# Other PSUM buffers for the turned x, and grams held next to their posts, in a kernel of RWKV-6 attention and an MLP-mixer

## The chip, the cores and the metric

The kernel runs on one core of one Trainium2 chip. The metric is the device time of one execution in microseconds (us), as the median of several runs. A program on one core has no die to compare with, so a run counts as fast when it is within 1.5% of the fastest run of its kernel. The engines are called as in the profile: PE is TensorE, PEld its weight loads, DVE is VectorE, ACT is ScalarE, SP is SyncE.

## The reference

Four batches of a recurrent attention are followed by an MLP-mixer. All inputs are fp32.

```python
# B=4, H=8 heads, S=768, D=48; d_model = 384
for t in range(S):
    cur = einsum('bhd,bhe->bhde', u[None] * kt, vt)
    y[:, :, t] = einsum('bhd,bhde->bhe', rt, state + cur)
    state = wt[:, :, :, None] * state + einsum('bhd,bhe->bhde', kt, vt)
x = y.transpose(0, 2, 1, 3).reshape(B, S, H * D)
# mixer: d_tok = 256, d_ch = 1536
h = maximum(x.transpose(0, 2, 1) @ w_tok1, 0) @ w_tok2
u = x + h.transpose(0, 2, 1)
out = u + maximum(u @ w_ch1, 0) @ w_ch2
```

The kernel works the recurrence in blocks. Within a piece of 256 tokens, six "levels" each compute a gram (products of k and r in small tiles of the TensorE array), and an engine picks the wanted entries out of it. A "post" then transposes k (kT), forms the state increments (kv), updates the states, and forms y from the states and from the picked grams. The mixer of one batch (h, turned x, z, q products) is woven with the attention of the next batch, so that small-tile and full-size products share TensorE.

## The kernel before

The program keeps its PSUM tiles in three pools, eight banks in all; a bank here is 512 columns of fp32 in the tiles as declared (a gram's is [128, 2, 512]). The names in quotes are the tags by which tiles share buffers.

```python
ps_g = ctx.enter_context(tc.tile_pool(name="ps_g", bufs=2, space=bass.MemoryType.PSUM))  # 2 x 2 banks: "gram"
ps_a = ctx.enter_context(tc.tile_pool(name="ps_a", bufs=1, space=bass.MemoryType.PSUM))  # 1 x 2 banks: kv, y: "a"
ps_m = ctx.enter_context(tc.tile_pool(name="ps_m", bufs=2, space=bass.MemoryType.PSUM))  # 2 x 1 bank: all else: "m"
```

The mixer's turning stage makes one h product and one turn of x for each of six chunks of 128 tokens. Both take an "m" buffer. VectorE empties the h buffer, ScalarE empties the turn's.

```python
def back(c):
    ps = ps_m.tile([128, DM], f32, name="h_ps", tag="m")
    for i in range(DTOK // 128):
        pe.matmul(ps, wtok2[:, i, ts(c, 128)], h1[:, i, :], ...)
    dve.tensor_add(x[:, c, :], x[:, c, :], ps)

def turn(c):
    ps = ps_m.tile([128, DM // 128, 128], f32, name="xT_ps", tag="m")
    for m in range(DM // 128):
        pe.transpose(ps[:, m, :], xs[bt][:, c, ts(m, 128)], ident)
    act.copy(xT[:, :, ts(c, 128)], ps)
```

The post's transposes of k also take "m" buffers, except in the first batch, where a gram buffer holds both halves.

```python
def tokens():
    ...
    if bt == 0:
        both = ps_g.tile([128, 2, 512], f32, name="gram").rearrange("p c (a t) -> p c a t", a=A)
    for c in range(UC):
        ps = both[:, c] if bt == 0 else ps_m.tile([128, A, 128], f32, name="kT_ps", tag="m")
        for a in range(A):
            pe.transpose(ps[:, a, :], k_[:, ts(c * A + a, 128)], ident)
        act.copy(L["kT"][:, c], ps)
```

One post is joined with the levels of the piece after it. A scheduler then decides the order on TensorE: it may place a gram's products in front of, among or behind the products that they are joined with.

```python
def one(*pieces):
    return (sum(c for c, _ in pieces), lambda: emit(pieces))

return [begin, tokens, one(carry, first), update, one(before, rest[0]), one(within, rest[1]), *loads, *rest[2:]]
```

Here `carry` makes kv, `first` the level-0 gram (gram0), `before` the part of y from the states, `rest[0]` the level-1 gram, `within` the part of y from the picked grams, `rest[1]` the level-2 gram.

## Time and profile before

| | before |
|---|---|
| time, median of 3 runs | 627.08 us (625.52 to 629.18) |
| span of the profiled run | 624.1 us |
| TensorE busy | 591.5 us, 95% |
| TensorE's share of the chain that ended last | 88% |
| VectorE's share of that chain | 6% |
| visits to the small tiles on TensorE (counted in the built order) | 86 |

The prediction below shows the page, the last batch's turning stage, a stretch with attention and a kT stage. One more place of the kernel before matters later: a turning stage of a middle batch, which has attention beside it. This is the chain in order of time; the columns are start in us, length in us, and what ran.

```profile
394.23 0.71 PE y_ps L370 x22
394.94 1.49 PE h_ps L428 x4
396.43 0.33 PE xT_ps L435 x3
396.76 0.38 PE y_ps L370 x16
397.13 1.50 PE h_ps L428 x4
```

TensorE never rests in these lines. Yet the y products come in scraps of 22 and 16, each scrap a visit to the small tiles of its own, and four h matmuls take 1.49 us instead of the 4 x 0.323 = 1.29 us of an undisturbed row. The scraps stand where an h product waits for an "m" buffer to be emptied. By the timeline ScalarE's copy of the turn came last at the first of these two h products (394.27 to 394.75 us), and VectorE's add at the second (396.47 to 397.02).

### The profile page before, as it was taken

The numbers are of one execution on the slowest core, as the hardware profiler recorded it, in microseconds if no ns is written. First come the engines' busy times: TensorE is split into PE (matmuls) and PEld (weight loads), VectorE is DVE, ScalarE is ACT, GpSimd is POOL, SyncE is SP. The second block draws the span as 40 slices with busy tenths as digits, with TensorE's granted clock in tenths as the row PEclk, the third lists the DMA queues.
The fourth block names the chain that finished last, engine by engine and source line by source line (L and its number), as shares of the span: only waits on it lengthen the run. The fifth ranks groups of instructions, "written<-read, shape, count | busy, mean of one in ns | idle before, by whom it ended". The sixth has DMA issues, their size and how long they took to land.

```text
span 624.1 us, 19852 instructions
## 1 busy us (share of the span) xinstructions
PE 591.5 (95%) x8980; PEld 500.7 (80%) x8980; DVE 341.5 (55%) x743; ACT 201.6 (32%) x500; POOL 7.2 (1%) x32
## 2 busy tenths in 40 slices
PE   2888788999999999999999999999999999999997
PEld 2867556876888896789889896789899885898987
DVE  5889799996766783436364362526243331040403
ACT  6064554520355433432323312332212411202020
POOL 4000000000000000000000000000000000000000
PEclk9996679999999999999999999999999999999999
DMA  8236564610232222111111100000000000000000
GB/s 344 105 80 213 162 197 141 221 43 27 65 94 79 54 67 66 30 50 27 53 45 60 27 28 27 1 2 3 26 2 27 2 27 1 0 1 26 16 12 26
DMA packets 19380, 38.63 MB, mean 62 GB/s; under 512 B 2112, under 2 KB 12864, under 8 KB 19296
## 3 DMA queue, kind: packets, MB, share of 16 engines
q1 hardware_dynamic: 19152, 37.36, 19.0%
q8 instruction: 70, 1.15, 0.8%
q14 instruction: 14, 0.11, 0.1%
q10 hardware_dynamic: 144, 0.00, 0.0%
HBM read 32.64 MB, written 4.72 MB: 60 GB/s over the span
## 4 chain that ended last, share of the span: by engine, by line
PE 88%; DVE 6%; ACT 3%; issue 1%; DMA 1%; SPq 0%; DVEq 0%; ACTq 0%
PE z_ps L443 30%; PE q_ps L477 25%; PE gram L256 8%; PE h_ps L428 5%; PE h_ps L421 5%; PE h_ps L453 3%; PE y_ps L383 2%; PE y_ps L370 2%; PE kv_ps L333 2%; PE gram L233 2%; PE kT_ps L323 1%; PE xT_ps L435 1%; PE gram L250 1%; DVE state L350 1%; DMA w<-in_rkw_dram 1%
## 5 line engine op out<-in xcount | busy, mean ns | idle before, releaser
L443 PE MATMUL z_ps<-xT,wch 128*128 128x256 f32 x864 | 195.3, 382 | 0.0
L443 PEld LDWEIGHTS z_ps<-xT,wch 128*128 128x128 f32 x864 | 161.4, 190 | 22.4 <-ACT z L445 0.7
L445 ACT ACTIVATE z<-z_ps 128x256 f32<-128x256 f32 x144 | 55.0, 382 | 159.4 <-PE z_ps L443 145.7
L477 PE MATMUL q_ps<-wch,z 128*128 128x192 f32 x528 | 93.6, 329 | 0.0
L477 PEld LDWEIGHTS q_ps<-wch,z 128*128 128x128 f32 x528 | 86.3, 190 | 1.3
L477 PE MATMUL q_ps<-scratch,z 128*128 128x192 f32 x396 | 71.1, 330 | 0.0
L256 PEld LDWEIGHTS gram<-r,k 48*64 48x64 f32 x3072 | 59.4, 153 | 13.0 <-issue 7.2
L256 PE MATMUL gram<-r,k 48*64 48x32 f32 x3072 | 64.6, 235 | 4.1 <-issue 1.8
L477 PEld LDWEIGHTS q_ps<-scratch,z 128*128 128x128 f32 x396 | 64.3, 190 | 0.9 <-ACT kT L324 0.2
L288 DVE TENSOR_TENSOR k<-k,decay 112x512 f32<-112x512 f32 x36 | 24.9, 691 | 46.1 <-PE gram L256 34.6
L469 DVE TENSOR_TENSOR z<-z 128x768 f32<-128x768 f32 x11 | 10.5, 958 | 63.5 <-ACT z L445 63.4
L288 DVE TENSOR_TENSOR k<-k,w 112x512 f32<-112x512 f32 x36 | 24.8, 690 | 35.6 <-PE gram L256 30.0
L428 PE MATMUL h_ps<-h,wtok 128*128 128x384 f32 x96 | 37.0, 510 | 3.8 <-DVE x L430 2.0
L350 DVE SCALAR_TENSOR_TENSOR state<-state,w_chunk,kv_ps 128x48 f32<-128x48 f32 x160 | 30.7, 258 | 17.3 <-PE kv_ps L333 17.3
L421 PE MATMUL h_ps<-x,wtok 128*128 128x384 f32 x96 | 37.5, 541 | 1.7 <-ACT x L389 1.6
L430 DVE TENSOR_TENSOR x<-x,h_ps 128x384 f32<-128x384 f32 x24 | 13.3, 555 | 36.6 <-PE h_ps L428 36.3
L233 PE MATMUL gram<-rp,kp 48*64 48x64 f32 x768 | 22.5, 248 | 10.9 <-ACT kp L221 8.2
L272 DVE COPY_PREDICATED at<-mask,gram 128x512 f32<-128x512 uint8 x36 | 32.3, 898 | 0.0
L233 PEld LDWEIGHTS gram<-rp,kp 48*64 48x64 f32 x768 | 18.4, 154 | 15.4 <-ACT kp L221 10.7
L421 PEld LDWEIGHTS h_ps<-x,wtok 128*128 128x128 f32 x96 | 19.2, 208 | 13.5 <-ACT x L389 2.0
L280 ACT COPY at<-gram 16x256 f32<-16x256 f32 x48 | 17.4, 363 | 36.3 <-PE gram L256 35.1
L428 PEld LDWEIGHTS h_ps<-h,wtok 128*128 128x128 f32 x96 | 16.4, 189 | 15.5 <-DVE x L430 3.3
(80 smaller groups left out, 563.0 us busy)
## 6 DMA issues: line engine op xcount, KB each, us to landing
scratch<-in_w_ch_dram SPq DMA_DIRECT2D x10, 512.0 KB, 4.4
vt<-in_v_dram SPq DMA_DIRECT2D x12, 384.0 KB, 3.7
out_dram<-o SPq DMA_DIRECT2D x24, 192.0 KB, 1.9
x<-in_w_ch_dram SPq DMA_DIRECT2D x8, 512.0 KB, 4.4
w<-in_rkw_dram SPq DMA_DIRECT2D x18, 192.0 KB, 3.3
k<-in_rkw_dram SPq DMA_DIRECT2D x18, 192.0 KB, 3.1
r<-in_rkw_dram SPq DMA_DIRECT2D x18, 192.0 KB, 3.5
scratch<-in_w_tok_dram SPq DMA_DIRECT2D x4, 512.0 KB, 9.2
```

The lines of the kernel that those rows point to most:

```text
L233: pe.matmul(g[cols, q, ts(a, T)], L["kp"][rows, tokens], L["rp"][rows, tokens], start=True, stop=True)
L256: fours(lambda q, j, rows, cols: pe.matmul(g[cols, q, ts(ca, 32)], k_[rows, ds(ca * 128 + j * T, T)], right[rows, ts(2 * ca + j, 32 // b), ...
L272: dve.copy_predicated(out=dst, data=g.rearrange("p q (m b) -> p q m b", b=b), mask=masks[l].rearrange("p x t -> p (x t)").rearrange("p (m ...
L280: act.copy(at[p:p + b, :, :, n * 2 * b + b:(n + 1) * 2 * b], g[p:p + b, :, :, ts(n, b)])
L288: dve.tensor_mul(left, left, wv[:, :, 1].unsqueeze(2).to_broadcast([ROWS, n, b]))
L350: dve.scalar_tensor_tensor(new[:, a], state[bt, g][:, a], L["w"][:, c, a, j:j + 1], got[:, a], op0=ALU.mult, op1=ALU.add)
L421: pe.matmul(sums[i], wtok1[:, c, ts(i, 128)], xs[bt][:, c, :], start=(c == 0), stop=(c == C - 1))
L428: pe.matmul(ps, wtok2[:, i, ts(c, 128)], h1[:, i, :], start=(i == 0), stop=(i == DTOK // 128 - 1))
L443: pe.matmul(ps, wch1[:, m, ts(jt, 128)], xT[:, m, ts(s, SEG)], start=(m == 0), stop=(m == DM // 128 - 1))
L445: act.activation(zs[s][:, jt, :], ps, AF.Relu)
L453: pe.matmul(ps, zs[0][:, jt, ts(n, 128)], wch2[:, jt, :], start=(jt == 0), stop=(jt == NJ - 1))
L477: pe.matmul(ps, a[:, j, :], b[:, j, :], start=(j == 0), stop=(j == HJ - 1))
```

## The change

It has two parts. The first moves the turned x out of the two "m" buffers: in the first and the last batch to the buffer of kv and y, in the middle batches to the gram buffers. The second holds a gram's products behind the last TensorE product of the piece that it is joined with, by a dependency in the scheduler that is declared `NoSync`. Its aim is one joint visit to the small tiles instead of several scraps.

```diff
+    block = nc.cur_bb.bb
+    no_sync = mybir.DependencyInfo(mybir.DependencyClass.NoSync, mybir.DependencyReason.DATA)
+
+    def products(f):
+        done = len(block.instructions)
+        f()
+        return [ins for ins in block.instructions[done:] if ins.engine == pe.engine]
 ...
         def turn(c):
-            ps = ps_m.tile([128, DM // 128, 128], f32, name="xT_ps", tag="m")
+            if bt in (0, B - 1):
+                ps = ps_a.tile([128, 2, 512], f32, name="xT_ps", tag="a")
+            else:
+                ps = ps_g.tile([128, 2, 512], f32, name="xT_ps", tag="gram")
+            ps = ps[:, 0, :DM].rearrange("p (m t) -> p m t", t=128)
 ...
+        def both(f, g):
+            behind = products(f)[-1].name
+            for ins in products(g):
+                tc.add_manual_dep(ins, behind, no_sync, reason="products in tiles together")
+
         def one(*pieces):
-            return (sum(c for c, _ in pieces), lambda: emit(pieces))
+            return (sum(c for c, _ in pieces), lambda: both(*(f for _, f in pieces)))
```

## The prediction

> **What bounds the kernel now.** I read the page first: busy shares, slices, chain by line.
>
> ```profile
> PE 591.5 (95%) x8980; PEld 500.7 (80%) x8980; DVE 341.5 (55%) x743; ACT 201.6 (32%) x500; POOL 7.2 (1%) x32
> PE   2888788999999999999999999999999999999997
> PEclk9996679999999999999999999999999999999999
> PE 88%; DVE 6%; ACT 3%; issue 1%; DMA 1%; SPq 0%; DVEq 0%; ACTq 0%
> ```
>
> TensorE is the bound from about 90 us on: 88% of the chain that ended last is TensorE, the granted clock is full there, VectorE is at 55%. But 95% busy does not mean that TensorE has nothing to lose. The chain in order of time shows what a matmul costs in a row: 72 z matmuls in 15.54 us (216 ns each), 84 q matmuls in 13.65 us (163 ns), 24 h matmuls in 7.74 us (323 ns), three transposes in 0.33 us. (One fp32 matmul of the program is two instructions, a transpose is one.) Anything above these is a wait or a change of tile size. Here is the last batch's turning stage (520 to 533 us) in that view; columns are start, length, what:
>
> ```profile
> 523.72 1.57 PE h_ps L428 x4
> 525.29 0.02 issue
> 525.31 0.56 DVE x L430
> 525.88 0.04 issue
> 525.92 1.57 PE h_ps L428 x4
> ```
>
> A chunk takes 525.92 - 523.72 = 2.20 us, while its work is 4 x 0.323 + 0.33 = 1.62 us. The missing 0.58 us is the next h product waiting for VectorE's add to empty its PSUM buffer: h products and turns alternate in the two "m" buffers, so each h product gets the buffer that the one before it just left. The timeline says the same: "idle 0.32" before that matmul, though its row counts as busy nearly throughout.
>
> Now a stretch with attention beside it:
>
> ```profile
> 194.92 2.79 PE z_ps L443 x12
> 197.70 1.08 PE y_ps L383 x64
> 198.78 0.92 PE gram L256 x64
> 199.70 2.79 PE z_ps L443 x12
> 202.49 1.06 PE gram L256 x64
> ```
>
> 64 small-tile products cost 1.06 to 1.08 us when they open a visit to the 64-row tiles, 0.92 us when they follow others; 12 z matmuls after a visit take 2.79, not 12 x 0.216 = 2.59 us. So one visit costs 0.14 + 0.20 = 0.34 us beyond its work. Last, a kT stage:
>
> ```profile
> 331.93 0.44 PE kT_ps L323 x4
> 332.37 0.26 PE gram L233 x2
> 332.63 0.59 PE kT_ps L323 x4
> 333.21 0.26 PE gram L233 x4
> 333.47 4.10 PE q_ps L477 x24
> ```
>
> Six gram instructions cost 0.52 us in two visits; inside a longer visit one costs about 0.0145 us (0.92/64).
>
> [...] here the h matmul's row says 510 ns while one starts each 323 ns. [...]
>
> **The change, part by part.** No operation is added or removed: 4574 matmuls in both programs. Comparing the two built orders, the changes between full and small tiles on TensorE fall from 173 to 127, so visits from 86 to 63. All orders are the same up to the first batch's turning stage (about 92 us).
>
> (a) Turns of the first and last batch move to the buffer of kv and y, free at that time. The h products then own both "m" buffers. Last batch: the stage runs from 520.29 to 533.15, 12.86 us; 24 x 0.323 + 18 x 0.109 = 9.71; of the difference 0.2 us is the restart at its head and stays: gain 2.95. First batch: from the first transposes (92.72) to the first z (103.73) 11.01 us; 16 x 0.323 + 18 x 0.109 = 7.13; gain 3.88. VectorE also converts weights here; laying its 0.55 us adds and 0.4 to 0.7 us conversions in the new order against chunks of 1.62 us, each add is ready before the turn that wants it (the add of a chunk has 1.62 us, a turn plus an h product). I take 3.8.
>
> (b) Turns of the two middle batches move to the gram buffers. Their waits were filled with scraps of gram and y, 22 instructions or so at a time. From first transposes to first z: 11.55 us (249.20 to 260.75) and 11.2 us (391.1 to 402.3). After: 7.13 + one visit of 48 y and 64 gram. Alone 48 y cost 1.06 as 64 do, gram behind them 0.92, restart 0.20: 2.2. That is 9.33 us. In the first of the two, 38 y of the next visit also come back from the scraps: +0.5; and one turn stands behind the gram's pick in the ring (k and r products and pick, 0.69 + 0.69 + 1.30 us, then an add of 0.55, against about 3.2 us of TensorE work): +0.3. Gains 1.4 and 1.85.
>
> (c) One visit in the first batch's attention (gram at 166.97, y at 168.88) becomes joint: 0.34.
>
> (d) Eight kT stages lose 15 small visits (14 fewer in the count, as one stays as part of a longer visit). At 0.34 us this would be 4.8 us, but I do not believe it: these scraps stand in waits. At 331.93 the second half of kT needs the buffer that VectorE's L503 (331.97, 0.35 us) empties: it could start at 332.40 by the timeline, against 332.56. The next q needs the buffer that ScalarE empties at 333.04, about 333.1 against 333.40. So 0.3 us of that stage is won. Done alike for the eight (three at 0.3, five at 0 to 0.1, those where kT waits for VectorE's k product or for a ScalarE queue full of picks): 1.15 us. The 112 gram instructions moved into the kv visits cost 112 x 0.0145 = 1.6 us there. Net -0.45.
>
> Sum: 2.95 + 3.8 + 1.4 + 1.85 + 0.34 - 0.45 = 9.9 us; 627.1 - 9.9 = 617.2 us.
>
> **Rivals.** First: (d) pays as designed, all visits at 0.34 us. For it: TensorE is the bound and the costs are exact to a hundredth. Against: the idle times named above. It would make 612 us. Second: held grams bring new waits. y must now come before its gram, and y waits for the state updates: where gram used to go first (218.79), y started at 219.43 just as VectorE ended the last update (219.4). In the new order it would be asked for at about 219.4, so 0 to 0.3 us each in three places; if the picks behind also slip, 2 to 3 us and 620. Third: the first batch's 3.8 us are given back, because VectorE is busy all of 104 to 135 us with conversions. Against: the last block of the first channel weight is written by 112.8 us, and the matmuls that read it start at about 124.5; the second weight is complete at 132.6, needed some 8 us after 135. Slack of over 8 us against 3.8. If wrong: 621. Fourth: sharing the gram ring stalls the turns of the middle batches (or the grams behind them), (b) gives nothing: 620.5.
>
> **Range and chances.** Rival one alone reaches 2% (below 614.5), and I give it one in ten. Slower by 2% would need 12 us of new waits that nothing in the orders shows. The runs of before spread over 3.7 us, so ±2 us is noise between sets. Range 613.8 to 620.6; faster by over 2% 0.09, within 2% 0.90, slower 0.01.
>
> **What would show it.** (a) The chain between 520 and 533 us should have no VectorE add, with chunks 1.62 us apart; likewise in the first batch. (b) One gram-and-y visit in each middle turning stage, and perhaps a short wait before the fifth turn of the second batch. (c, d) kT stages of eight transposes in a row with a wait between the halves and one behind, of 0.2 to 0.4 us, about as long as the scraps were; kv and gram in one visit of about 2.2 us. Wrong would be: kT stages without those waits (then 612), or new idle time before y or before turns (then 620).

## The result, and the profile after

| | before | after |
|---|---|---|
| time, median of 6 runs each on one chip | 626.71 us (625.52 to 629.18) | 618.60 us (617.19 to 619.60) |
| ratio of fast runs | | 0.9865, 95% interval 0.9843 to 0.9887 |
| span of the profiled run | 624.1 us | 617.1 us |
| visits to the small tiles | 86 | 63 |

A ratio here is the mean time of one kernel's fast runs over the mean of the other's in the same rounds, so it is not quite the ratio of the medians quoted beside it. 1.35% is less than 2%; the interval shows that the gain is real. The predicted time was 617.2 us and the range 613.8 to 620.6.

First the page of the kernel after: busy time by engine, the granted TensorE clock in 40 slices, and the shares of the chain that ended last.

```profile
PE 587.0 (95%) x8980; PEld 499.0 (81%) x8980; DVE 341.2 (55%) x743; ACT 201.1 (33%) x500; POOL 7.2 (1%) x32
PEclk9999679999999999999999999999999999999999
PE 86%; DVE 6%; ACT 3%; DMA 2%; issue 2%; SPq 0%; ACTq 0%; DVEq 0%
```

The busy share of TensorE is 95% as before, although 7 us of the span are gone. The share tells nothing of this change, because a part of the waits counts as busy: of the 0.58 us missing in each chunk of the prediction's turning stage, only 0.32 show as idle. The counts of these instructions are the same; the granted clock is 1.00 from 90 us on in both (windows of 90 to 617 us here and of 90 to 623 us before).

The last batch's turning stage, chain in order of time:

```profile
519.32 1.29 PE h_ps L437 x4
520.61 0.33 PE xT_ps L449 x3
520.94 1.29 PE h_ps L437 x4
522.23 0.33 PE xT_ps L449 x3
```

Chunks are 520.94 - 519.32 = 1.62 us apart instead of 2.20, VectorE's add is no longer in the chain, and four h matmuls take the 1.29 us of an undisturbed row.

The middle batch's turning stage (the one shown above of before):

```profile
395.84 0.33 PE xT_ps L449 x3
396.17 0.89 PE y_ps L379 x42
...
397.23 0.93 PE gram L265 x59
398.15 0.48 PE xT_ps L449 x3
```

The scraps of y and gram have become one visit, with y first and gram behind it (where they meet, a few start times mix).

A kT stage:

```profile
330.56 0.45 PE kT_ps L332 x4
...
331.09 0.59 ACT kT L333
...
331.73 4.17 PE q_ps L491 x24
```

The grams that stood here before are gone, and nothing has taken their place. The q product after the transposes waits until ScalarE's copy (331.09 to 331.69) has emptied the "m" buffer of the first half. TensorE needs 0.44 us for each half, so it is idle for 331.73 - 330.56 - 0.88 = 0.29 us by this chain.

Two more places matter. The first is before y:

```profile
188.94 0.64 DVE at L248
189.58 0.32 DVE state L359 x2
189.90 0.64 DVE at L248
190.55 1.55 DVE state L359 x9
...
192.24 1.15 PE y_ps L379 x64
193.38 0.92 PE gram L265 x62
```

y now has to come before its gram, and it waits for VectorE's state updates, which stand in the chain with the two picks of gram0 (L248) among them. The second place is a later gram of the attention:

```profile
226.69 0.99 PE gram L265 x57
227.67 0.22 issue
227.90 0.32 PE gram L265 x7
```

The last seven of the gram's 64 products start late; by the usual spacing of such products the hole is 0.43 us. The profile names nothing that they waited for ("issue").

### The profile page after: what moved, and what is told of

Read it like the earlier page. It is cut to its first block, busy times and chain, and to the rows that moved or that the text cites. A ratio compares the mean times of both kernels' runs of the same rounds, so it can differ in the third digit from the quotient of the medians.

```text
span 617.1 us, 19869 instructions
## 1 busy us (share of the span) xinstructions
PE 587.0 (95%) x8980; PEld 499.0 (81%) x8980; DVE 341.2 (55%) x743; ACT 201.1 (33%) x500; POOL 7.2 (1%) x32
## 4 chain that ended last, share of the span: by engine, by line
PE 86%; DVE 6%; ACT 3%; DMA 2%; issue 2%; SPq 0%; ACTq 0%; DVEq 0%
PE z_ps L457 28%; PE q_ps L491 24%; PE gram L265 8%; PE h_ps L430 6%; PE h_ps L437 5%; PE h_ps L467 3%; PE y_ps L392 2%; PE kv_ps L342 2%; PE y_ps L379 2%; PE gram L242 1%; PE xT_ps L449 1%; PE gram L259 1%; ACT at L276 1%; DMA scratch<-in_w_ch_dram 1%; DMA w<-in_rkw_dram 1%
## 5 line engine op out<-in xcount | busy, mean ns | idle before, releaser
L430 PE MATMUL h_ps<-x,wtok 128*128 128x384 f32 x96 | 39.3, 562 | 2.0 <-ACT x L398 1.7
L437 PE MATMUL h_ps<-h,wtok 128*128 128x384 f32 x96 | 35.5, 494 | 0.1
L242 PE MATMUL gram<-rp,kp 48*64 48x64 f32 x768 | 18.0, 245 | 10.8 <-ACT kp L230 8.0
L298 DVE TENSOR_TENSOR r<-r,w 112x512 f32<-112x512 f32 x36 | 24.6, 686 | 5.7 <-ACT rp L226 5.7
L242 PEld LDWEIGHTS gram<-rp,kp 48*64 48x64 f32 x768 | 15.9, 155 | 12.6 <-ACT kp L230 10.5
```

The costliest lines, as they stand in the source:

```text
L242: pe.matmul(g[cols, q, ts(a, T)], L["kp"][rows, tokens], L["rp"][rows, tokens], start=True, stop=True)
L298: dve.tensor_mul(right, right, wv[:, :, 0].unsqueeze(2).to_broadcast([ROWS, n, b]))
L430: pe.matmul(sums[i], wtok1[:, c, ts(i, 128)], xs[bt][:, c, :], start=(c == 0), stop=(c == C - 1))
L437: pe.matmul(ps, wtok2[:, i, ts(c, 128)], h1[:, i, :], start=(i == 0), stop=(i == DTOK // 128 - 1))
```

## The experiments

Eight kernels, one of them the kernel after once more, ran in two sets, each on a chip of its own and with five rounds, all with correct results. The kernel before, run in between, had a median of 626.04 us (11 runs, 624.45 to 627.36) in the first set and 626.15 us (11 runs, 624.20 to 627.66) in the second. The first four rows of the table are the first set. "Visits" are counted in the built orders.

| kernel | median us | ratio to before | 95% interval | visits |
|---|---|---|---|---|
| turns_only | 616.16 | 0.9843 | 0.9826 to 0.9860 | 78 |
| hold_only | 627.98 | 1.0031 | 1.0017 to 1.0045 | 69 |
| loose_gram0 | 617.81 | 0.9858 | 0.9837 to 0.9879 | 77 |
| kT_in_kv_buffer | 610.48 | 0.9757 | 0.9738 to 0.9776 | 63 |
| after_again | 617.27 | 0.9862 | 0.9841 to 0.9882 | 63 |
| loose_y | 617.95 | 0.9866 | 0.9844 to 0.9887 | 63 |
| kT_kv_no_hold | 610.84 | 0.9757 | 0.9736 to 0.9777 | 64 |
| kT_kv_only | 621.71 | 0.9927 | 0.9908 to 0.9945 | 73 |

The theory behind the set: the turns' buffers make the whole gain, and the hold of the grams makes nothing, because scraps of gram only filled waits that stay. The rival: each visit saved is worth 0.34 us, so that the hold carries its part.

**turns_only** is the kernel after with the first part of the change alone.

```diff
 def one(*pieces):
-    return (sum(c for c, _ in pieces), lambda: both(*(f for _, f in pieces)))
+    return (sum(c for c, _ in pieces), lambda: emit(pieces))
```

> The new buffers for the turns, without holding products together. Theory (the buffers made the whole gain, and the hold cost a little): the four turning stages keep their 9.9 us, the scraps of gram return to the kT stages and fill waits there, so 617 to 618.5 us, at or up to 1.5 us below the changed kernel; 78 visits to the small tiles instead of 63 cost nothing on balance. Rival (each avoided visit is worth its 0.34 us): 15 more visits make it 5 us slower than the changed kernel, 623 to 624 us.

It has 15 visits more than the kernel after and is not slower: 0.9843 against 0.9862 in the set after it, just below the time that I expected. Its trace, counted from the start of the first h product, is 9.85 us shorter than that of before. Its four turning stages gain 3.6, 1.58, 1.88 and 2.94 us, 10.0 us together. That is the whole gain.

**hold_only** is the second part alone.

```diff
 def turn(c):
-    if bt in (0, B - 1):
-        ps = ps_a.tile([128, 2, 512], f32, name="xT_ps", tag="a")
-    ... (gram buffer in the middle batches)
+    ps = ps_m.tile([128, DM // 128, 128], f32, name="xT_ps", tag="m")
```

> The products held together, with the turns back in the two m buffers. Theory: the waits for the add in the first and last batch stay, visits fall from 86 to 69, but most of those visits stood in waits, so 625 to 627 us, at most 1.5 us below the kernel before. Rival: 17 visits at 0.34 us make it 5.8 us faster, 621 us.

It removes 17 visits and is 0.31% slower than the kernel before, with an interval that excludes zero: about 1.9 us lost, where the rival's count would have won 17 x 0.34 = 5.8 us. My own theory missed too, as it allowed no loss. Its last batch shows that the turning stage is untouched; chain in order of time:

```profile
525.47 1.57 PE h_ps L437 x4
...
527.06 0.56 DVE x L439
...
527.67 1.57 PE h_ps L437 x4
```

The chunks are 2.20 us apart with VectorE's add between them, as in the kernel before.

**loose_gram0** keeps both parts, but gram0 is not held behind kv.

```diff
-        return [begin, tokens, one(carry, first), update, ...
+        return [begin, tokens, (carry[0] + first[0], lambda: emit((carry, first))), update, ...
```

> The changed kernel, but gram of level 0 is not held behind kv; the other two pairs still are. Theory: 14 visits come back at the kT stages, where they fill waits; the early batch wins about 1 us, the later ones lose about 0.5 us: 617.5 to 618.5 us, within 1 us of the changed kernel. Rival: 14 visits at 0.34 us, 4.8 us slower, 623 us.

Fourteen visits come back, and the time is that of the kernel after (0.9858 against 0.9865 and 0.9862, all intervals overlapping). So the 14 visits that come back cost nothing that shows; they lie in waits. Its trace has one thing more to teach. The waits before y, which measured 0.17, 0.24 and 0.29 us in the kernel after, are gone: the only one left is 0.08 us. (The same profile has three holes like the one shown above, of 0.25, 0.28 and 0.74 us, so its span doesn't show the gain.)

**kT_in_kv_buffer** takes away the wait itself. From the second batch on, kT gets the two-bank buffer of kv and y, which is free at that time: y of the piece before has been copied out, and kv can only start when kT has been copied out.

```diff
             if bt == 0:
                 both = ps_g.tile([128, 2, 512], f32, name="gram").rearrange("p c (a t) -> p c a t", a=A)
+            else:
+                both = ps_a.tile([128, 2, 512], f32, name="kT_ps", tag="a").rearrange("p c (a t) -> p c a t", a=A)
             for c in range(UC):
-                ps = both[:, c] if bt == 0 else ps_m.tile([128, A, 128], f32, name="kT_ps", tag="m")
+                ps = both[:, c]
```

> The changed kernel, with k turned in kv's own two-bank buffer from the second batch on, so that neither half of kT nor the product behind it waits for an m buffer. Theory (the waits that took the place of the scraps are waits for the two m buffers): the waits between the halves (2.0 us summed over the nine stages of the changed kernel's trace) and behind them (1.9 us) go, with most of the 0.1 us restarts: 613.5 to 615.5 us. Rival (these stages wait for VectorE's and ScalarE's chain of picks, not for buffers): the time comes back at the next product, 617.5 to 619 us.

Of the first set it is the only kernel that is faster by more than 2%: 610.48 us. The gain on the kernel after is 6.8 us by the medians (after_again has 617.27), more than the 3 to 5 us that I had allowed. A kT stage of it, chain in order of time:

```profile
326.54 0.44 PE kT_ps L334 x4
326.98 0.98 PE q_ps L493 x6
327.95 0.44 PE kT_ps L334 x4
328.39 2.93 PE q_ps L493 x18
```

The two halves of kT no longer wait for one another's buffers: a whole q product (6 x 0.163 = 0.98 us) fits between them, and no line is longer than its work. I compared the spacing of TensorE's instructions around all kT stages after the first batch with their undisturbed spacing. The kernel after waits 6.60 us there in all, this kernel 0.85 us. The 5.75 us between them are the larger part of the gain. They also explain the miss: the theory counted the waits between the halves and behind them (2.0 and 1.9 us) and left out those before the first half, 2.9 us in the kernel after and 0.5 us here.

**after_again** is the kernel after, unchanged, to stand beside the second set.

> The changed kernel once more, on the chip and in the rounds of the three runs beside it, as their measure: 617.5 to 619.5 us. Its profile also shows how long the head takes whose order of instructions is the same in all kernels here (start of the first h product of the mixer at 89.5 us before, 91.4 us in the changed kernel's first profile, 90.0 to 92.3 in four others). Theory (the head differs from run to run, not from kernel to kernel): somewhere from 89.5 to 92.3 us. Rival (the change made it longer): 91.4 us again.

The ratio is 0.9862, against 0.9865 in the first measurement. So the sets can be compared. The head of its profile takes 90.6 us, where the first profile of the same program has 91.4.

**loose_y** keeps both parts, but the level-1 gram is not held behind the states' part of y. My theory was that the new waits before y would go, for 0.4 to 1.2 us.

```diff
-        return [..., update, one(before, rest[0]), one(within, rest[1]), *loads, *rest[2:]]
+        return [..., update, (before[0] + rest[0][0], lambda: emit((before, rest[0]))), one(within, rest[1]), *loads, *rest[2:]]
```

> The changed kernel, but the level-1 gram is not held behind y's state products; kv with gram 0 and y's second half with gram 2 stay held. The visits are 63 as in the changed kernel, only the order inside three of them differs (25, 10 and 3 gram products come before y). Theory (part of the hold's cost is that y is asked for before its state is there): the waits before y of 0.17, 0.24 and 0.29 us and part of those around 226 us go: 0.4 to 1.2 us below the changed kernel, about 617.5. Rival (the hold's cost lies in the kT stages alone): equal to the changed kernel within 0.2 us.

The theory fell: the time is that of the kernel after, and the waits are still there. By the spacing of instructions the three waits before y are 0.58, 0.24 and 0.42 us, where the kernel after has 0.17, 0.24 and 0.29. This is the first of them in the timeline of TensorE; the columns are start, busy time, engine, line, operation, tiles and count, and the bracket is the idle time before it with what ended it.

```profile
164.79 1.00 PE L265 MATMUL gram<-r,k 48*64 48x32 f32 x50
...
166.17 0.96 PE L379 MATMUL y_ps<-state,r 48*64 48x48 f32 x42 [0.38 <-DVE state L359]
```

Now 50 gram products stand in front of y, and y still waits for the state update. So it is not the hold of this gram that makes y wait. The hold of gram0 is: loose_gram0, which drops that hold alone, has 0.08 us of these waits left. The other kernels agree: hold_only has all three waits (0.17, 0.24 and 0.30 us), turns_only a single one of 0.19 us. The chain shown above of the kernel after suggests how: with gram0 directly behind kv, VectorE gets its two picks of 0.64 us among the state updates that y waits for. That the picks' place does it is argued from the chain, not tried alone.

**kT_kv_no_hold** is kT_in_kv_buffer without the hold (that is, turns_only with kT in the kv buffer). I expected 609 to 610 us if the hold still cost something.

```diff
 (the edit of kT_in_kv_buffer, and)
 def one(*pieces):
-    return (sum(c for c, _ in pieces), lambda: both(*(f for _, f in pieces)))
+    return (sum(c for c, _ in pieces), lambda: emit(pieces))
```

> Turns and kT in the new buffers, nothing held. Theory (with no waits for buffers left, there is nothing for scraps to fill, so the scheduler leaves the products together by itself): 64 visits against 63 with the hold, no kT scraps, no early y: 0.5 to 1.5 us below the same kernel with the hold, 609 to 610 us. Rival (the hold pays once the buffers no longer hide it): slower than with the hold, 611 us or more.

It took 610.84 us, so that gain did not come; the ratio is that of the kernel with the hold, 0.9757. Where kT has its own buffer, the hold is worth nothing in either direction that these runs could show. The waits around kT are 0.84 us here and 0.85 us with the hold, and the visits 64 and 63: with no waits left to fill, the scheduler makes no scraps by itself.

**kT_kv_only** is the kernel before with kT in the kv buffer, and neither part of the change. I expected 618 to 620 us.

```diff
 (the edit of kT_in_kv_buffer, applied to the kernel before)
```

> The kernel before with kT in kv's buffer alone. Theory (buffer waits at the kT stages and at the turning stages are separate costs that add): the 8 us that kT's buffer gave the changed kernel less what the hold had cost there, so 6 to 8 us below the kernel before: 618 to 620 us. Rival (the two share one cause, relief of the m buffers anywhere is enough): 623 us or more.

It took 621.71 us, 4.4 us below before, so the expectation missed by about 2 us; the rival's 623 us lies above all six runs (at most 622.6). An account from the traces agrees with it within the interval: 13 visits fewer at 0.34 us are 4.4 us, and the open waits around kT fall from 1.64 to 0.81 us. Together that is an estimate of 5.2 us, and the interval (0.9908 to 0.9945 of 626 us) spans 3.4 to 5.8 us. The effects of the two buffer moves multiply: 0.9927 x 0.9843 = 0.977, where kT_kv_no_hold measured 0.9757 with an interval from 0.9736 to 0.9777.

## Why the prediction was right, point by point

The prediction was right in its time: 618.6 us measured, 617.2 us predicted. By its own steps, each stage measured from its first transposes to the end of the stage in both traces:

| step | predicted gain, us | measured gain, us |
|---|---|---|
| (a) turns, first batch | 3.8 | 3.59 |
| (a) turns, last batch | 2.95 | 2.94 |
| (b) turns, second batch | 1.4 | 1.40 |
| (b) turns, third batch | 1.85 | 1.80 |
| (c) and (d) together | 0.34 - 0.45 = -0.11 | -0.81 (-0.56 in after_again) |

**(a) and (b) were right.** The arithmetic was to replace the stage's length by the undisturbed spacing of its matmuls, and to put the small-tile visit back where there is one. It held to 0.05 us in three stages. In the first batch 0.2 us were lost again in waits of z behind the stage. The short wait before the fifth turn of the second batch exists, but is about 0.1 us (a turn of 0.43 instead of 0.33 us at 258.11), not 0.3; so the exact 1.40 of that stage is partly luck, as other terms must make up for it. One reading was too narrow: in the first batch four of the five waits of the kernel before ended with ScalarE's copy of the turn (such as 0.49 us at 93.09, just before an h product), not with VectorE's add. The change removes both, so the sum did not suffer. In the last batch the gap of about 0.58 us came back from chunk to chunk, and another buffer, with no other edit (turns_only), gained 2.94 us in that stage, as much as the whole change does.

**(d) was right in its mechanism.** Rival one, that each visit pays 0.34 us, is refuted by hold_only and loose_gram0. The late kT stages gained what was predicted: 0.30, 0.30 and 0.31 us in three, 0.09 us in another. The account of all kT stages after the first batch shows why so little: before, 1.64 us of open waits and 14 more visits, which are 14 x 0.34 = 4.8 us, stood there, 6.4 us in sum; after, 6.60 us of open waits stand there. The scraps were paid for by waits of the same length. The wait is the cost, the scrap only its filling.

**What was mis-sized is the term for (c) and (d) in the sum: it left out new waits.** Rival two named them before y, at 0 to 0.3 us in each of three places, but the sum took them as zero. They measured 0.17, 0.24 and 0.29 us, 0.70 in all (the same to 0.01 in after_again), where the kernel before had only one, of 0.19 us: 0.51 us lost. With the kT stages (6.4 us and 1.6 us of grams before, 6.60 after: a gain of 1.4), the grams moved to kv (-1.6) and the joint visit (+0.34), the sum is 1.4 - 1.6 + 0.34 - 0.51 = -0.37 us.

The rest is the hole in a gram, 0.43 us in this profile: -0.80, where -0.81 was measured. In after_again the hole is not there; another, of 0.33 us, stands in an earlier gram (-0.70, where -0.56 was measured). As the same program has it at different places, its place belongs to the run. Whether the change makes such holes likelier is open: five of the seven profiles with the turns moved have at least one of over 0.2 us, none of the three with the turns in the "m" buffers. The views put the holes down to "issue", but the DMA records of the traces hold a lead. The eight holes of that size stand at only three places in TensorE's order (within four instructions), and each ends 1.36 to 1.57 us after one of the 70 transfers of 16,384 bytes in the queue that the page calls "instruction" has landed. Whether the two are connected is not shown: other profiles pass the same places as soon after such a transfer and have no hole, and no run changes it. Since the visits enter with an average cost, agreement to a few hundredths is partly luck.

In the timed runs, the hold costs 1.0031 alone (a loss with an interval clear of zero), 0.9862 against 0.9843 beside the turns' buffers (about 1.2 us, intervals overlapping), and nothing once kT has its buffer.

**Rivals three and four did not happen.** VectorE's conversions did not take back the first batch's gain (3.59 of 3.8 us stayed), and the shared gram ring did not stall the middle turns.

**The head of the kernel is noise that the prediction did not name.** The order of TensorE's instructions is the same in all kernels up to about 92 us, but the first h product starts between 89.5 us (before) and 92.3 us (kT_in_kv_buffer) in the ten profiles. The profile of the kernel after lost 1.9 us there, which is why its span is only 7.0 us shorter, while the rest of it gained 8.9 us. The granted clock in that stretch differs between runs (from 40 to 60 us it was 0.74 in before and 1.00 in the kernel after), and profiles with the same time at half clock (0.50 granted) have nearly the same head: 90.6 to 90.8 us in the three with 13.7 us at half clock, 91.3 and 91.4 in the two with 17.1, 89.5 to 90.0 in the three with 27.3 (before is one), 90.9 with 30.2 and 92.3 with 34.1. So the two go together, though more time at half clock is not always a longer head. Which drives the other is not shown; the cause stays open. One profile of each kernel would have misled by a fifth of the effect; the timed ratios, 0.9865 and 0.9862, agree.

The gain was some 8.5 us by the ratio (1.35% of 626.7) and 8.1 us by the medians, not 9.9. The base was 626.0 to 626.7 us in the later sets, not the prediction's 627.1; by the medians this hid 0.4 us of the miss.

## What to carry to other kernels

Where TensorE is 95% busy, as here, compare the spacing of its instructions in the chain with their undisturbed spacing. What was above it in these traces was a wait (about 0.58 us in a chunk of the last batch, of which 0.32 showed as idle), a visit to the small tiles (0.34 us), or a hole of unknown cause (0.25 to 0.74 us); waits were also filled with scraps of other work. Do not tidy the scraps away; find which buffer the wait is for, and give the tile another buffer that is free at that time. Here that rule gave 9.8 us for the turned x and, applied once more to the transposed k, some 5 to 7 us more (610.5 us, the best version, with or without the hold), while holding the products together gave nothing or cost up to 1.9 us.

## Costs measured in these traces

- A visit to the 64-row tiles cost 0.34 us beyond its work: 0.14 us on the 64 small products that open it (1.06 against 0.92 us), and 0.20 us on the 12 full-size z matmuls behind it (2.79 against 2.59 us). Fewer visits were not faster by themselves: 17 fewer made hold_only 0.31% slower than the kernel before.
- The hand-over of one buffer, from the end of an h product (128x384 fp32) to the start of the product that waits for its buffer, was 0.02 + 0.56 + 0.04 = 0.62 us through VectorE (525.29 to 525.92 us before). For a 128x512 copy by ScalarE it was about 0.72 us (331.01 to 331.73 us after).
- For 256, 192 and 384 columns of fp32, TensorE's matmul instructions in a row were 216, 163 and 323 ns apart. One fp32 matmul of the program is two such instructions, and a transpose is one: 4574 matmuls, 168 of them transposes, are 8980 instructions.
